# k and v in whole-batch loads and a first stage in another order, in an attention and token-mixing kernel on one NeuronCore

## The chip, the cores and the metric

The kernel runs on one core of a Trainium2 chip. The metric is the device time of one launch in microseconds (us). The core has a matrix engine (TensorE, PE in the profile, with its weight loads shown as PEld), a vector engine (VectorE, DVE), a scalar engine (ScalarE, ACT), a general engine (GpSimd, POOL) and a queue engine (SyncE, SP) that here only starts transfers (DMA). Each engine takes its instructions in program order and waits on semaphores for others.

## The reference

Inputs are float32: q, k, v with 8 batches, 8 heads, 576 rows and 64 columns, a gain `g_norm`, and four weight matrices.

```python
kv = np.einsum('bhsd,bhse->bhde', k, v)
out = np.einsum('bhsd,bhde->bhse', q, kv)
rms = np.sqrt(np.mean(out * out, axis=-1, keepdims=True) + 1e-06)
x = out / rms * g_norm                 # then heads side by side: (8, 576, 512)
...
xt = x.transpose(0, 2, 1)
h = np.maximum(xt @ w_tok1, 0.0) @ w_tok2        # 576 -> 256 -> 576 over rows
u = x + h.transpose(0, 2, 1)
h2 = np.maximum(u @ w_ch1, 0.0) @ w_ch2          # 512 -> 1536 -> 512 over columns
return u + h2
```

The weights arrive as 64-bit numbers; the kernel turns them into float32 itself.

## The kernel before

*Stages.* The batches are worked in four pairs. For each pair there is an attention stage and a token-mixing stage, and these are interleaved: while pair p is mixed, the attention of pair p+1 runs beside it. After the four pairs come the two large channel products, which hold PE for most of the time and which the change leaves alone.

*Order.* Nothing is scheduled by the compiler: every instruction is recorded in program order (`keep`), and the order is written out by hand in lists of short names (`start`, `middle`, `steady`, lines 1241 on) which `play` runs from left to right. `start` is the first stage: the attention of pair 0, the decoding of the token weights, and the first half of the token mixing of pair 0 (batch 0). `middle` follows: the rest of it, for batch 1, and the attention of pair 1. Each name adds instructions to one or several engines; each engine then sees only its own, in that order. The names:

- `kv{s}{h}`: the 64x64 products of k and v for side s (batch) of the pair and half h of its eight heads, 20 matmuls into `ps_kv`. `e{s}{h}` copies them to SBUF (`kvp`), on DVE in pair 0, on ACT later.
- `a{c}{t}`: tile t of chunk c is attended, four 128x128 matmuls into `ps_o` (two buffers). Chunks 0 and 1 are batch 0, chunks 2 and 3 batch 1, chunk 4 is the remainder of 64 rows of both. From pair 1 on an attend is `a{c}`, made of 64x64 matmuls.
- `g`, `q`, `t` for the same tile: gain (DVE multiplies `ps_o` by `g_norm` into x), square (ACT, from `ps_o` to `sq`), total (DVE sums the squares by head). A square follows its gain, since both read the bank, and the bank is free for the next attend after the square.
- `m`, `r`, `i` for a chunk: mean (DVE), root (ACT), inverse (four small DVE instructions).
- `s`, `p`, `d` for a tile: x times the inverse, on ACT (eight instructions of 64 columns), on POOL (one instruction of 512) or on DVE (one of 512). All three are there to choose from.
- `h{s}{t}`: the first token product for side s and half t of the 256 outputs, four 128x512 matmuls into `ps_h`; `h0{t}{j}` is one of these four, for row tile j. `hr` adds the remainder rows. `u{i}` is the second token product.
- `w{n}1` to `w{n}4`: decoding of token weight block n: ACT scales both halves of each number, DVE clamps, shifts and adds. Blocks 0 and 1 are the two halves of `w_tok1`, 2 its remainder rows, 3 and 4 `w_tok2`.
- `l`, `lq`, `lr`: loads of k and v, of q, of q's remainder rows for a later pair.
- `j{n}`: n matmuls of the identity with itself, into a bank that nobody reads (`keep_warm`).

*Loads.* `load(n)` brings half the heads of one batch of k and of v: 512 rows in 128x4 pieces of 256 columns (1 KB each), and 64 rest rows. There are four buffers of k and four of v, so a pair fills all of them. The first two loads of v start on ACT's queue, all others on SP's. Eight semaphores serve the loads on SP and ACT in turn, so a transfer waits until the one eight issues ahead of it has landed. Ahead of `start`, in this order: load 0, the two halves of the token weights, load 1, q of batch 0, loads 2 and 3, q of batch 1, the remainders, the other token weights.

Of the kernel before, what the change touches and what calls it, by code (L numbers as in the profile page):

```python
# [11 lines left out]
F32 = mybir.dt.float32  # L12
# [8 lines left out]
def kernel(  # L21
# [32 lines left out]
    nc = tc.nc  # L54
    P = 128
    B, S, DM = k.shape
    D = g_norm.shape[0]
# [3 lines left out]
    J, JJ, HF = 4, 5, 64  # L61
    LO = P * J
# [3 lines left out]
    DH = DM // 2  # L66
# [11 lines left out]
    def pool(name, bufs, side="left", stack=ctx, **kw):  # L78
        return stack.enter_context(tc.tile_pool(name=name, bufs=bufs, side=side,
                                                reuse_waits="tile", **kw))  # L80
# [9 lines left out]
    inp = pool("inp", 1, "left", left)  # L90
# [12 lines left out]

    w_ch1 = w1p.tile([P, 4, 4, FQ], F32, name="w_ch1")
    w_ch2 = w2p.tile([P, 4, NS, DH], F32, name="w_ch2")
    k_in = [inp.tile([P, JJ, DH], F32, name=f"k_in{i}") for i in range(4)]
    v_in = [inp.tile([P, JJ, DH], F32, name=f"v_in{i}") for i in range(4)]
    kvp = [inp.tile([P, HP, P], F32, name=f"kvp{i}") for i in range(2)]
    u_rest = dram.tile([J * P, DM], F32, name="u_rest")
    u_rows = lambda u: u_rest if u == B else out[u, :LO]  # L110
# [1 line left out]
    def do(f, *a, **kw):  # L112
        return lambda: f(*a, **kw)
# [6 lines left out]
    def dma(o, i, engine=nc.sync):  # L120
        keep(engine.dma_start(o, i))
# [10 lines left out]
    def matmul(*a, **kw):  # L132
        keep(nc.tensor.matmul(*a, **kw))  # L133
# [1 line left out]

    qT, q_rest = {}, {}

    def load(n):

        if n >= 2 * B:  # L140
            return
        cols = [t[n // 2, :, ts(n % 2, DH)] for t in (k, v)]

        queues = (nc.sync, nc.scalar if n < 2 else nc.sync)
        for dst, c, e in zip((k_in[n % 4], v_in[n % 4]), cols, queues):
            dma(dst[:, :J], c[:LO].rearrange("(j p) e -> p j e", p=P), e)
            dma(dst[:HF, J], c[LO:], e)

    def load_q(b):
        if b < B:  # L150
            qT[b] = qtp.tile([P, HP, LO], F32, name="qT", tag="qT", bufs=2)
            dma(qT[b], q[b].rearrange("(c p) s -> p c s", p=P)[..., :LO])
# [69 lines left out]
    def get_ch2(f):  # L222

        a = 2 * (2 * f // NS)

        def loads(raw):
            t = raw.rearrange("p (h f n) w -> p f h n w", h=2, f=2)
            rows = words(moe_w_ch2)[ts(f, 2 * P)].rearrange("(f p) (h n) w -> f p h n w", f=2, h=2)
            return [(t[:, i], rows[i]) for i in range(2)]

        dst = w_ch2[:, a:a + 2, ds(2 * f % NS, 2)]
        return block(2 * DM, loads, dst.rearrange("p h f n -> p h (f n)"))
# [121 lines left out]
    def attention(pair, groups):  # L354
# [7 lines left out]
        whole = pair == 0  # L362

        def kv(side, half):
            n = 4 * pair + 2 * side + half
            kk, vv = k_in[n % 4], v_in[n % 4]
            if whole:
                o = kv_ps[side, half] = zeroed[half]
            else:
                o = kv_ps[side, half] = ps["kv"].tile([P, 2, P], F32, name="ps_kv", tag="kv")  # L370
            for i in range(2):
                for j in range(JJ):
                    for h in range(2):
                        at = ds(i * P + h * D, D)
                        matmul(o[ds(h * D, D), i, ds(h * D if whole else 0, D)], lhsT=kk[:, j, at],
                               rhs=vv[:, j, at],
                               start=(j == 0), stop=(j == JJ - 1), skip_group_check=True)
# [130 lines left out]
        steps = {}  # L508
        for s in range(2):
            for h in range(2):  # L510
                steps |= {f"kv{s}{h}": do(kv, s, h), f"e{s}{h}": do(evict, s, h),
                          f"l{s}{h}": do(load, 4 * pair + 4 + 2 * s + h)}
            steps |= {f"lq{s}": do(load_q, 2 * pair + 2 + s), f"lr{s}": do(load_q_rest, 2 * pair + 2 + s)}
        for c in range(5):
            if whole:
# [676 lines left out]
    def play(lines, after={}, **stages):  # L1192
# [3 lines left out]
        for name in " ".join(lines).split():  # L1196
# [5 lines left out]
            else:  # L1202
# [6 lines left out]
    channel = ([get_ch1(c, f) for f in range(2) for c in range(NC)]  # L1209
               + [get_ch2(f) for f in range(NF // 2)])  # L1210
    load(0)
    for block in tok1[:2]:
        block[0]()
    load(1)
    for t in [t for pair in zip(k_in, v_in) for t in pair]:
        keep(nc.gpsimd.memset(t[HF:, J], 0.0))
    zeroed = [ps["kv"].tile([P, 2, P], F32, name="ps_kv", tag="kv") for _ in range(2)]
    for t in zeroed:
# [5 lines left out]
    make_identity(nc, ident)  # L1224
    dma(g_sb, bass.AP(tensor=g_norm.tensor, offset=g_norm.offset,
                      ap=[[0, P], [0, 1], list(g_norm.ap[0])]), nc.scalar)
    load_q(0)
    for n in range(2, 4):
        load(n)
    load_q(1)  # L1230
    load_q_rest(0)
    load_q_rest(1)
    for block in tok1[2:] + tok2:
# [5 lines left out]


    start = [
        "kv00 e00 l00 j14 w01 w11 w02 w03 w04 w12 w13 w14", "kv01 j10 e01 l01",
        "a00 g00 q00", "a01 g01 q01 t00", "a10 g10 q10 t01 m0 r0", "a11 g11 q11 t10 i0 p00 p01",
        "kv10 j6 t11 m1 r1 e10 i1 s10 p11", "kv11 j2 e11", "h000 h001 h002 h003", "a20 g20 q20", "a21 g21 q21 t20",
        "h010 t21 m2 r2", "a30 g30 q30 i2 p20", "a31 g31 q31 t30", "h011 t31 m3 r3 p21", "a40 i3 p30 g40 q40 p31",
        "h012 h013 t40 m4 r4 w21 i4 s40 lq0 l10 l11 lr0 lr1"]
    middle = [
        "kv00 e00 w31 w22 w23 w24", "h10 -lq1 w32 w33 w34", "kv01 e01 w41 w42",
        "h11 w43 w44", "hr l00", "a0 q00 g01 q01 g00 t00 t01", "u0 z2 f0", "u1 l01",
        "a1 q10 g11 q11 g10 t10 t11 m0 r0 lq0", "u2 i0", "kv10 e10 z4 d00", "u3 s01", "kv11 e11",  # L1250
        "u4 z6 f1", "a2 q20 g21 q21 g20 s10", "u5 t20 t21 f2", "a4 q40 g41 q41 g40 lr0 lr1 1", "u6 t40 t41 1 l10",
        "a3 q30 g31 q31 g30 lq1 d11", "u7 t30 t31 m2 r2 1 i2 p20 p21 s30", "u8 1 l11 d31"]
    steady = [[
        "kv00 kv01 e00 e01 1 -d40 f3", "h00 1 x00", "h01 1 f4 b00", "a0 q00 g01 q01 g00 l00 1",
        "h10 t00 t01 1 x01", "h11 l01 1 x10 b01", "hr 1 x11 z2 f5 f6", "a1 q10 g11 q11 g10 lq0", "kv10 kv11 e10 e11 t10 t11 m0 r0",
        "u0 i0 1", "u1 1 d00 l10", "u2 s01 z4 1 f7", "a2 q20 g21 q21 g20", "u3 s10 t20 t21",
        "u4 z6 l11", "a4 q40 g41 q41 g40 lr0 lr1 1", "u5 d11 t40 t41 1", "a3 q30 g31 q31 g30 lq1",
        "u6 t30 t31 m2 r2 i2 d20 p21 s30", "u7 1 d31 1", "u8 1 b10 b11"], [
        "kv00 kv01 e00 e01 1 -d40 f8", "h00 1 x20", "h01 1 f9", "a0 q00 g01 q01 g00",
        "h10 t00 t01 1 x21", "h11 1", "hr 1 z2 f10", "a1 q10 g11 q11 g10", "kv10 kv11 e10 e11 t10 t11 m0 r0",  # L1260
# [2 lines left out]
        "u6 t30 t31 m2 r2 i2 d20 p21 s30", "u7 1 d31 b20 b21", "u8 f13"]]  # L1263

    attentions = [attention(0, ((0,), (1,), (2,), (3,), (4,)))]
    attentions += [attention(p, ((0, 1), (2, 3, 4))) for p in range(1, B // 2)]

    mixings = [token_mixing(p, (2, 4, 6)) for p in range(B // 2 - 1)]
# [135 lines left out]
```

## The time and the profile before

| what | us |
|---|---|
| median of 3 runs | 789.2 (789.14 to 789.29) |
| the profiled execution, its own time | 788.88 |
| its span, first to last instruction | 787.1 |
| PE busy | 774.4 (98%) |
| DVE, ACT, POOL busy | 612.9, 265.4, 78.3 |
| moved by DMA | 192.12 MB, mean 244 GB/s |

The profile is one execution of the program. It gives for each engine which instruction ran when, what it waited for, and how long a transfer took from its issue to its landing. The time of a launch is about 1.8 us longer than the span in it. In the profile's names `ps_kv<-v_in,k_in` is a kv product, `ps_o<-kvp,qT` an attended tile, `ps_h<-x,w_tok` a first token product, `ps_j<-ident` the identity products. One float32 matmul appears as two records. Instructions of helper functions carry the helper's line: L133 is `matmul`, L121 `dma`.

How far transfers lie apart at the start: load 0, started at 0.75 us, lets the first kv begin at 6.24; the q of batch 0, started at 7.5, lands 9.1 us later.

### The profile page before, as it was taken

The page shows a single profiled execution, that of the slowest core. Times are in us where ns is not written, and L with a number is a line of the kernel's source. Part 1 is how long each engine was busy: PE and PEld are TensorE (multiplying, and loading weights), DVE is VectorE, ACT ScalarE, POOL GpSimd, SP SyncE. Part 2 cuts the span into 40 slices and gives each one's busy share as a digit, 9 for nine tenths or more (in the row PEclk, how much of TensorE's full clock was granted, in tenths as well). Part 3 has the DMA queues.
Part 4 walks back from the last instruction along what each step waited for, and adds up shares of the span by engine and source line. Part 5 has one row for each costly group of instructions (what it writes and reads, how often), then busy time and mean ns, then how long its engine had stood idle before and what let it go on. Part 6 is the DMA issues. An engine that isn't in the chain of part 4 may idle for free.

```text
span 787.1 us, 14853 instructions
## 1 busy us (share of the span) xinstructions
PE 774.4 (98%) x5832; PEld 652.6 (83%) x5832; DVE 612.9 (78%) x906; ACT 265.4 (34%) x513; POOL 78.3 (10%) x91
## 2 busy tenths in 40 slices
PE   6999999999999999999999999999999999999998
PEld 5655555544888888999988899998889999889998
DVE  2666887796776868988778889776898885787977
ACT  2356564846110133511133242123352113325211
POOL 1211212122410000010100001010000101000111
PEclk9999999999999999999999999999999999999999
DMA  9999999587699795599897579889559889655864
GB/s 295 327 334 371 361 371 344 212 268 282 235 292 337 269 339 148 154 309 205 246 236 231 151 218 272 247 203 290 148 158 283 206 222 230 200 153 151 200 173 91
DMA packets 132614, 192.12 MB, mean 244 GB/s; under 512 B 13633, under 2 KB 92225, under 8 KB 132545
## 3 DMA queue, kind: packets, MB, share of 16 engines
q1 hardware_dynamic: 115984, 167.54, 68.1%
q0 software_dynamic: 14656, 22.02, 13.7%
q10 hardware_dynamic: 1904, 1.61, 0.7%
q8 instruction: 46, 0.75, 0.4%
q14 instruction: 24, 0.19, 0.1%
HBM read 138.31 MB, written 52.82 MB: 243 GB/s over the span
## 4 chain that ended last, share of the span: by engine, by line
PE 95%; DVE 2%; ACT 1%; DMA 1%; issue 0%; SPq 0%; ACTq 0%
PE ps_d L133 28%; PE ps_b L133 19%; PE ps_a L133 19%; PE ps_h L133 8%; PE ps_u L133 8%; PE ps_v L133 5%; PE ps_c L133 3%; PE ps_kv L133 2%; PE ps_w L133 2%; PE ps_o L133 2%; DMA raw<-in_moe_w_tok_dram 1%; ACT x L498 1%; DVE x L444 0%; DVE ms L465 0%; PE ps_j L133 0%
## 5 line engine op out<-in xcount | busy, mean ns | idle before, releaser
L133 PE MATMUL ps_d<-ui,w 128*128 128x256 f32 x504 | 118.6, 379 | 0.0
L133 PEld LDWEIGHTS ps_d<-ui,w 128*128 128x128 f32 x504 | 95.1, 190 | 12.8 <-DVE v L124 0.2
L130 ACT COPY ps_d<-ps_a 128x768 f32<-128x768 f32 (+1 forms) x56 | 32.0, 571 | 215.6 <-PE ps_a L133 215.6
L124 DVE TENSOR_TENSOR v<-v,v 128x1536 f32<-128x1536 f32 (+2 forms) x70 | 103.5, 1483 | 0.3
L133 PE MATMUL ps_b<-w,sv 128*128 128x128 f32 x672 | 84.7, 276 | 0.0
L133 PE MATMUL ps_a<-w,v 128*128 128x128 f32 x672 | 84.2, 275 | 0.0
L133 PEld LDWEIGHTS ps_a<-w,v 128*128 128x128 f32 x672 | 79.9, 192 | 0.2
L133 PEld LDWEIGHTS ps_b<-w,sv 128*128 128x128 f32 x672 | 79.5, 192 | 0.2
L133 PE MATMUL ps_u<-h,w_tok 128*128 128x512 f32 (+1 forms) x160 | 67.2, 606 | 0.2
L133 PE MATMUL ps_d<-w,v 128*128 128x128 f32 x528 | 66.3, 275 | 0.0
L133 PE MATMUL ps_h<-x,w_tok 128*128 128x512 f32 (+1 forms) x160 | 65.5, 603 | 0.7 <-ACT x L498 0.7
L133 PEld LDWEIGHTS ps_d<-w,v 128*128 128x128 f32 x528 | 62.7, 192 | 0.3
L127 ACT ACTIVATE v<-v 128x768 f32<-128x768 f32 (+1 forms) x54 | 42.6, 821 | 55.1 <-DVE v L124 55.1
L133 PE MATMUL ps_d<-w,sv 128*128 128x128 f32 x480 | 60.1, 275 | 0.0
L133 PEld LDWEIGHTS ps_d<-w,sv 128*128 128x128 f32 x480 | 57.1, 192 | 0.2
L133 PEld LDWEIGHTS ps_h<-x,w_tok 128*128 128x128 f32 (+1 forms) x160 | 26.1, 189 | 32.7 <-issue 29.0
L1121 POOL DMA_DIRECT2D out_dram<-us x11 | 14.1, 1278 | 379.3 <-ACT us L130 347.4
L133 PEld LDWEIGHTS ps_u<-h,w_tok 128*128 128x128 f32 (+1 forms) x160 | 24.8, 179 | 31.0 <-issue 25.6
L133 PE MATMUL ps_a<-uT,w 128*128 128x256 f32 x192 | 46.7, 379 | 0.0
L444 DVE TENSOR_TENSOR x<-ps_o,g_sb 128x512 f32<-128x512 f32 x32 | 21.6, 687 | 28.6 <-PE ps_o L133 23.3
L133 PE MATMUL ps_b<-ui,w 128*128 128x256 f32 x168 | 40.8, 379 | 0.0
L133 PEld LDWEIGHTS ps_a<-uT,w 128*128 128x128 f32 x192 | 36.3, 190 | 4.8
(145 smaller groups left out, 1216.2 us busy)
## 6 DMA issues: line engine op xcount, KB each, us to landing
w<-parts SPq DMA_DIRECT2D x168, 384.0 KB, 4.1
w<-parts SPq DMA_DIRECT2D x56, 192.0 KB, 3.4
uT<-blocks SPq DMA_DIRECT2D x36, 256.0 KB, 5.7
k_in<-in_k_dram SPq DMA_DIRECT2D x16, 512.0 KB, 8.7
qT<-in_q_dram SPq DMA_DIRECT2D x8, 1024.0 KB, 9.2
out_dram<-x POOLq DMA_DIRECT2D x16, 512.0 KB, 6.1
v_in<-in_v_dram SPq DMA_DIRECT2D x14, 512.0 KB, 8.8
raw<-in_moe_w_ch_dram SPq DMA_DIRECT2D x8, 768.0 KB, 10.4
```

What stands on the lines that cost most here:

```text
L124: keep(engine.tensor_tensor(out=o, in0=a, in1=b, op=op))
L127: keep(nc.scalar.activation(o, a, AF.Relu))
L130: keep(nc.scalar.copy(o, a))
L133: keep(nc.tensor.matmul(*a, **kw))
L444: keep(nc.vector.tensor_mul(x, bank[c, h], g_sb.to_broadcast([P, number(c), D])))
L498: keep(nc.scalar.activation(x[:, k, h], x[:, k, h], AF.Copy, scale=inv[:, k, h]))
L1121: keep(nc.gpsimd.dma_start(to.rearrange("t p e -> p t e"), a, accum_op=ALU.add))
```

## The change

k and v are loaded for whole batches, in pieces of 512 columns (2 KB), into two buffers each; `l{s}` replaces `l{s}0` and `l{s}1`, and kv picks its half inside the buffer. q of batch 0 is loaded right after k of batch 0, in front of the token weights; only v of batch 0 is on ACT's queue. The list `start` is new: both kv of batch 0 come first, the identity products are 6 and 14 instead of 14, 10, 6 and 2, the token weights are decoded between the gains of the first tiles, tiles are scaled by DVE (`d`) and ACT (`s`) where POOL (`p`) did seven of nine, and kv of batch 1 comes after the first token products. In `middle`, `h10` stands ahead of `kv00`.

```diff
-    k_in = [inp.tile([P, JJ, DH], F32, name=f"k_in{i}") for i in range(4)]
-    v_in = [inp.tile([P, JJ, DH], F32, name=f"v_in{i}") for i in range(4)]
+    k_in = [inp.tile([P, JJ, DM], F32, name=f"k_in{i}") for i in range(2)]
+    v_in = [inp.tile([P, JJ, DM], F32, name=f"v_in{i}") for i in range(2)]
...
-    def load(n):
-
-        if n >= 2 * B:
-            return
-        cols = [t[n // 2, :, ts(n % 2, DH)] for t in (k, v)]
-
-        queues = (nc.sync, nc.scalar if n < 2 else nc.sync)
-        for dst, c, e in zip((k_in[n % 4], v_in[n % 4]), cols, queues):
-            dma(dst[:, :J], c[:LO].rearrange("(j p) e -> p j e", p=P), e)
-            dma(dst[:HF, J], c[LO:], e)
+    def load(b):
+
+        if b < B:
+            for t, dst, queue in ((k, k_in, nc.sync), (v, v_in, nc.sync if b else nc.scalar)):
+                dma(dst[b % 2][:, :J], t[b, :LO].rearrange("(j p) e -> p j e", p=P), queue)
+                dma(dst[b % 2][:HF, J], t[b, LO:], queue)
...
         def kv(side, half):
-            n = 4 * pair + 2 * side + half
-            kk, vv = k_in[n % 4], v_in[n % 4]
+            kk, vv = k_in[side], v_in[side]
...
-                        at = ds(i * P + h * D, D)
+                        at = ds(half * DH + i * P + h * D, D)
...
-                steps |= {f"kv{s}{h}": do(kv, s, h), f"e{s}{h}": do(evict, s, h),
-                          f"l{s}{h}": do(load, 4 * pair + 4 + 2 * s + h)}
+                steps |= {f"kv{s}{h}": do(kv, s, h), f"e{s}{h}": do(evict, s, h)}
+            steps[f"l{s}"] = do(load, 2 * pair + 2 + s)
...
     load(0)
+    load_q(0)
     for block in tok1[:2]:
         block[0]()
-    load(1)
...
-    load_q(0)
-    for n in range(2, 4):
-        load(n)
+    load(1)
     load_q(1)
...
     start = [
-        "kv00 e00 l00 j14 w01 w11 w02 w03 w04 w12 w13 w14", "kv01 j10 e01 l01",
-        "a00 g00 q00", "a01 g01 q01 t00", "a10 g10 q10 t01 m0 r0", "a11 g11 q11 t10 i0 p00 p01",
-        "kv10 j6 t11 m1 r1 e10 i1 s10 p11", "kv11 j2 e11", "h000 h001 h002 h003", "a20 g20 q20", "a21 g21 q21 t20",
-        "h010 t21 m2 r2", "a30 g30 q30 i2 p20", "a31 g31 q31 t30", "h011 t31 m3 r3 p21", "a40 i3 p30 g40 q40 p31",
-        "h012 h013 t40 m4 r4 w21 i4 s40 lq0 l10 l11 lr0 lr1"]
+        "kv00 e00 kv01 e01 j6", "a00 w01 g00 q00", "a01 w02 w03 g01 q01 t00 w04 w11 t01 m0 r0",
+        "a10 g10 q10 i0 d00 d01", "a11 w12 w13 g11 q11 t10 w14", "j14 h000 h001 t11 m1 r1 l0", "h010 h011 i1 d10 s11",
+        "kv10 e10 kv11 e11", "h002 h012 a20 g20 q20", "a21 g21 q21 t20 h003 h013 t21 m2 r2 lq0", "a30 g30 q30 i2 d20 s21",
+        "a31 g31 q31 t30 t31 m3 r3", "a40 g40 q40 i3 s30 d31 t40 m4 r4 w21 i4 s40 l1 lr0 lr1"]
     middle = [
-        "kv00 e00 w31 w22 w23 w24", "h10 -lq1 w32 w33 w34", "kv01 e01 w41 w42",
-        "h11 w43 w44", "hr l00", "a0 q00 g01 q01 g00 t00 t01", "u0 z2 f0", "u1 l01",
+        "h10 w31 w22 w23 w24 -lq1", "kv00 e00 w32 w33 w34", "kv01 e01 w41 w42",
+        "h11 w43 w44", "hr l0", "a0 q00 g01 q01 g00 t00 t01", "u0 z2 f0", "u1",
...
```

In the rest of `middle` and in `steady`, `l0` stands where `l00` stood, `l1` where `l10` stood or two products ahead of it, and `l01` and `l11` are gone.

## The prediction

> **What bounds the kernel now.** I read the busy table first, then who TensorE (PE) waits for, then the timeline of its first 52 us, then the stretches of the span.
>
> The page, then PE's waits over the whole span (engine, line, releaser; us in total, times, longest):
>
> ```profile
> span 787.1 us, 14853 instructions
> PE 774.4 (98%) x5832; PEld 652.6 (83%) x5832; DVE 612.9 (78%) x906; ACT 265.4 (34%) x513; POOL 78.3 (10%) x91
> PE   6999999999999999999999999999999999999998
> ...
> PE ps_kv L133 <- DMA v_in<-in_v_dram: 6.2, 1, 6.2
> PE ps_kv L133 <- DVE w_tok L178: 1.1, 1, 1.1
> PE ps_o L133 <- ACT sq L448: 0.8, 2, 0.5
> PE ps_h L133 <- ACT x L498: 0.7, 1, 0.7
> ```
>
> PE is the bound, and of its 12.7 us of idleness the 6.2 before the first matmul is half. The page's first slice (6, then 9s) says the same: all that can be won or lost lies at the start. Stretches (length, then busy time of PE, PEld, DVE, ACT, POOL, clock, DMA share, GB/s):
>
> ```profile
> 2.50:6.24 3.74, 0.00 (x1) 0.03 (x1) 0.00 (x0) 1.49 (x2) 0.79 (x4) 1.00 1.06 331
> ...
> 13.98:16.59 2.61, 2.61 (x53) 2.54 (x50) 1.39 (x3) 0.00 (x0) 0.00 (x0) 1.00 1.06 375
> ...
> 46.05:127.00 80.95, 80.59 (x1049) 42.75 (x1046) 63.68 (x126) 49.96 (x121) 13.73 (x17) 1.00 1.07 361
> ...
> 500.00:787.10 287.10, 283.85 (x1989) 268.21 (x1987) 230.28 (x298) 79.90 (x141) 18.11 (x15) 1.00 0.75 198
> ```
>
> From 46.05 to 500 PE is idle for 0.5 us; the 3.25 missing in the last stretch is the end of the kernel, which the change does not touch. DMA is full in the same first 127 us, but PE does not wait for it after the first loads. So the prediction is one number: when PE reaches the first attend of pair 1 (51.60), from which its queue is full. PE's timeline:
>
> ```profile
> 6.24 2.40 PE L133 MATMUL ps_kv<-v_in,k_in 128*64 128x64 f32 x40 [6.24 <-DMA v_in<-in_v_dram]
> 8.57 4.07 PE L133 MATMUL ps_j<-ident 128*128 128x128 f32 x28
> 13.77 1.39 PE L133 MATMUL ps_kv<-v_in,k_in 128*64 128x64 f32 x40 [1.14 <-DVE w_tok L178]
> 15.09 2.50 PE L133 MATMUL ps_j<-ident 128*128 128x128 f32 x20
> 17.42 1.95 PE L133 MATMUL ps_o<-kvp,qT 128*128 128x128 f32 x16
> ...
> 31.22 1.95 PE L133 MATMUL ps_o<-kvp,qT 128*128 128x128 f32 x16
> 33.00 1.02 PE L133 MATMUL ps_h<-x,w_tok 128*128 128x512 f32 x2
> 33.86 1.95 PE L133 MATMUL ps_o<-kvp,qT 128*128 128x128 f32 x16
> 35.65 1.02 PE L133 MATMUL ps_h<-x,w_tok 128*128 128x512 f32 x2
> ...
> 39.79 1.39 PE L133 MATMUL ps_kv<-v_in,k_in 128*64 128x64 f32 x40
> 41.10 3.70 PE L133 MATMUL ps_h<-x,w_tok 128*128 128x512 f32 x8
> ```
>
> Start to start this prices everything on PE: a kv of 20 matmuls (40 records) 1.31 us, the first one 2.33; one attended tile 0.89; one 128x512 product 0.91; a dummy record 0.117 (20 in 2.33).
>
> And the scaling on ACT:
>
> ```profile
> 27.33 2.02 ACT L498 ACTIVATE x<-x,inv 128x64 f32<-128x64 f32 x8 [1.28 <-DVE inv L484]
> ```
>
> **What the Trainium skill says.** "TensorE: Matmul & The Clock Gate", Part 1, has the array at half clock until some 3.4 us of activity, and again after an idle window of that length. The trace agrees with the first half: 2.33 against 1.31, and the dummies are slow until about 10.0, so 3.8 us; no gap in it is long enough to show the second half. The same page (its paragraph on engine queue depths) says ACT and DVE queues are strictly in order; the timelines show nothing else. "VectorE: DVE Perf Modes", section on the TRN2 errata, charges every small instruction a fixed latency: the eight 64-column scalings cost 2.02, one 512-column multiply on DVE 0.69. "DMA: Bandwidth & Descriptors", "Issuing engines are not separate DMA queues": SP's and ACT's transfers share 16 engines, so two doubled loads at once take twice as long.
>
> **The change part by part.** All times below are a schedule by hand with the durations above, instructions in the order that the built program of the changed kernel has.
>
> *Whole-batch loads.* The first kv needs 1.05 MB before (main parts of half k and half v), 2.10 after. The extra 1.05 MB takes 2.8 us at 375 GB/s (a stretch in which a q load of 2 KB rows moves), and 2 KB rows save some of the first part (331 to 375: 0.4). First matmul at about 6.24+2.8-0.4, taken as 8.5; bounds 7.5 and 9.2. Later loads are wider and half as many; they lie beside a full PE, so they are worth nothing, and their buffers (two where there were four halves) are refilled after the second half is read, 20 us or more before use. SP has 30 issues fewer (60 to 30); PE does not wait for its issue time. POOL's eight clearings of 0.31 become four of twice the width, done before 4, ahead of the first kv.
>
> *kv00 and kv01 together.* Slow for 3.8 us: 2.33 + 1.47 slow, rest 0.5, to 12.8; six dummies (1.4) to 14.2. q, now in front of the token weights, has 1.05 MB behind 2.36: lands near 12, hidden by these. First attend at 14.2 instead of 17.42: 3.2 won, and 12 of 32 dummies gone.
>
> *First tiles.* DVE's gain of a tile starts 1.1 after its attend, ACT's square follows it (0.69, 0.60), and only then is the bank free. g00 15.3 to 16.0; a10 waits for its square, 16.7. DVE now decodes token weights between the gains (w02 w03, 0.9), so g01 ends at 17.6, its square at 18.25, a11 18.3 to 19.2. Fourteen dummies (3.3) to 22.5. Token weights land near 13.5 and 15.2 (0.52 MB each at 310 GB/s), before ACT reads them.
>
> DVE in order: t00, w04, t01, m0 to 19.7 (0.65+0.69+0.65+0.18); g10 20.35; i0 (root and four small ops) 21.35; d00 and d01, which POOL did in 2.04, 0.7 each to 22.7; w12 w13 23.6; g11 24.25; t10 24.9; w14 25.5. The second token product waits for w14 in the built program: h000 22.5 to 23.4, then 2.1 idle, to 25.55. POOL's scaling stood beside DVE; here decode and scaling queue on DVE: that is the first loss.
>
> *Middle of the stage.* h001 h010 h011 28.3; kv10 kv11 30.9 (their loads land near 21: slack); h002 h012 32.7; a20 a21 34.5, at which the kernel before was at 33.0 (31.22+1.78). The gain of 3.2 is spent. h003 h013 36.3; a30 a31 38.1.
>
> *The last wait.* g20 to 34.5, its square and g21, q21 36.05, t21 36.8, m2; g30 holds DVE to 38.1; i2 39.0; s21 on ACT 39.05 to 41.05. q31, the square of tile 31, was ready at 40.4 but is queued behind these eight scalings: 41.05 to 41.6. t31 42.3, m3 and root 42.85, g40, i3 44.15, s30 44.2 to 46.2. PE meanwhile: remainder 39.8, h10's first product 40.7, second (after s21) 41.95, third needs s30: idle 4.3 to 46.25. Before, the like chain from a31 (about 35.6) to the end of POOL's p31 (42.57) is 6.9 long; mine is 8.1, and h10 now stands ahead of kv00, so kv00 and kv01 (2.6) no longer cover it.
>
> *Sum.* h10's last two 1.8: 48.05; kv00 kv01 50.7; h11 3.6: 54.3; the four remainder products 1.9: 56.2. Before 51.60. Later by 4.6, and nothing after it has idle time to absorb this. Ledger: start +2.3, slow part of the second kv +0.7, dummies 4.7 for 8.3, so -3.6, wait for w14 +2.1, last wait +4.3, short waits (a10, a11 and the remainder 0.7 each, s21 0.3) +2.4, waits of before -3.5 (the 2.6 listed, and about 0.2 at each of the five that the modelled end of the matmul ahead hides): 4.7, the same within rounding.
>
> The execution profiled took 788.88 for a span of 787.1; the median shown is 789.2. 787.1+4.6 is a span of 791.7, a time of 793.5 on that execution and 793.8 on the median.
>
> **Rivals.** *Slower still:* the 4.3 us of idleness ends in half clock, as the skill has it for a window of 3.4; price as at the start, 3.8 us of half-speed work, 1.9: 795.7. Against it: an idle stretch barely over the window need not fill one.
> *No difference:* the last wait is short, because squares and scalings interleave better than I lay out or s30 comes before PE gets there: 793.8-4.3 = 789.5. For it: before, such chains end just in time; against it, 6.9 measured.
> *Faster:* the 3.2 us won at the first attend stay won. It needs both waits, 2.1 and 4.3, filled, deciding where w14 ends before 23.4 and s30 before 42: 793.8-6.4 = 787.4. For it: 3.6 us of dummies less and the earlier attend are sure; against it, DVE's list from 14.2 to 25.5 has under 1 us of slack.
> *The wider rows do something later:* PE's 0.5 us of waits between 46 and 500 is all they can win.
>
> **How the numbers follow.** Slower by my chain 0.67, by it with half clock 0.18, no difference 0.08, faster 0.07. This kernel's measurement tells 0.2%, 1.6 us, from no change. So slower 0.85, same 0.08, faster 0.07. Predicted 793.8. Range: first load from 7.5 to 9.2 moves it by -1.0 to +0.7, handovers of some 0.05 over about 20 steps by another 1, half clock by +1.9: 791.6 to 796.6; the cases left out hold under 0.2.
>
> **What would show it.** First matmul 8 to 9; first attend near 14; waits of PE for the token decode (about 2) and for ACT's x scaling in the last products of pair 0 (about 4, releaser L493 in the changed file); DMA GB/s higher up to 127 us without effect; the first 64x64 attend near 56. I am wrong if that attend stands at or before 52, or if PE has new gaps after it.

## The result, and the profile after

| | before | after |
|---|---|---|
| median, us | 789.2 | 798.85 (796.74 to 799.39) |
| ratio of after to before | | 1.0114, 95% interval [1.0098, 1.013] |
| span of the profiled execution, us | 787.1 | 797.1 |
| PE busy, us | 774.4 | 774.6 |
| DVE, ACT, POOL busy, us | 612.9, 265.4, 78.3 | 615.7, 269.5, 71.2 |
| first kv, first attend, a0 of pair 1, us | 6.24, 17.42, 51.60 | 11.83, 18.15, 61.66 |

The change makes the kernel slower by 1.1%, about twice what was predicted, and outside the range. The new 10 us of the span are all there when PE reaches a0 of pair 1, 10.06 later than before. From there to the end both kernels take the same 735.4 to 735.5 us (length of the stretch first; the changed kernel's line stands below, with its other stretches). The kernel before:

```profile
51.60:787.10 735.50, 731.77 (x5410) 621.68 (x5408) 586.84 (x841) 246.94 (x468) 68.35 (x70) 1.00 0.81 239
```

PE's timeline of the changed kernel (start and length in us, engine, line, operation, records, and in brackets the idle time ahead with its releaser):

```profile
11.83 4.63 PE L133 MATMUL ps_kv<-v_in,k_in 128*64 128x64 f32 x80 [11.83 <-DMA v_in<-in_v_dram]
16.39 1.92 PE L133 MATMUL ps_j<-ident 128*128 128x128 f32 x12
18.15 1.95 PE L133 MATMUL ps_o<-kvp,qT 128*128 128x128 f32 x16
...
23.01 3.29 PE L133 MATMUL ps_j<-ident 128*128 128x128 f32 x28
26.13 1.02 PE L133 MATMUL ps_h<-x,w_tok 128*128 128x512 f32 x2
28.86 2.84 PE L133 MATMUL ps_h<-x,w_tok 128*128 128x512 f32 x6 [1.71 <-DVE w_tok L174]
31.64 2.55 PE L133 MATMUL ps_kv<-v_in,k_in 128*64 128x64 f32 x80
...
42.99 2.33 PE L133 MATMUL ps_h<-x,w_tok 128*128 128x512 f32 x4
49.11 3.78 PE L133 MATMUL ps_h<-x,w_tok 128*128 128x512 f32 x4 [3.79 <-ACT x L493]
52.82 3.35 PE L133 MATMUL ps_kv<-v_in,k_in 128*64 128x64 f32 x80
56.11 5.62 PE L133 MATMUL ps_h<-x,w_tok 128*128 128x512 f32 x16
61.66 1.16 PE L133 MATMUL ps_o<-kvp,qT 64*64 64x64 f32 x64
```

The first kv begins 5.6 us later, yet the first attend only 0.7 later, since six identity products stand ahead of it where there were 24. The rest is lost between first attend and a0 of pair 1, which takes 43.5 us where it took 34.2.

PE's waits over the whole span of the changed kernel (releaser; us in total, times, longest):

```profile
PE ps_kv L133 <- DMA v_in<-in_v_dram: 11.8, 1, 11.8
PE ps_h L133 <- ACT x L493: 3.8, 1, 3.8
PE ps_h L133 <- DVE w_tok L174: 1.7, 1, 1.7
PE ps_o L133 <- ACT sq L443: 1.0, 3, 0.5
PE ps_r L133 <- ACT sq L443: 0.6, 1, 0.6
```

Between first attend and a0 of pair 1 these are 6.8 us: 3.79, 1.71, 0.58, and 0.76 of the waits for `sq`, whose third comes later. Before, the waits in the same place were 1.4:

```profile
19.89 2.05 PE L133 MATMUL ps_o<-kvp,qT 128*128 128x128 f32 x16 [0.52 <-ACT sq L448]
...
29.40 1.98 PE L133 MATMUL ps_h<-x,w_tok 128*128 128x512 f32 x4 [0.73 <-ACT x L498]
...
36.85 1.09 PE L133 MATMUL ps_r<-kvp,qR 128*64 128x128 f32 x16 [0.18 <-ACT sq L448]
```

The stretches around the longest wait (length, busy time of PE, PEld, DVE, ACT, POOL, granted clock, DMA share, GB/s), again of the changed kernel:

```profile
42.99:49.11 6.12, 2.25 (x6) 0.59 (x4) 4.69 (x12) 4.51 (x18) 0.00 (x0) 0.89 1.07 334
49.11:52.82 3.71, 3.71 (x4) 1.18 (x4) 1.72 (x8) 3.44 (x13) 0.00 (x0) 0.50 1.10 316
52.82:56.11 3.29, 3.29 (x82) 3.22 (x81) 1.58 (x3) 0.78 (x2) 0.00 (x0) 0.73 0.22 82
56.11:61.66 5.55, 5.55 (x21) 2.13 (x17) 1.68 (x3) 2.13 (x4) 0.00 (x0) 1.00 0.81 247
61.66:797.10 735.44, 731.72 (x5410) 621.76 (x5408) 586.95 (x841) 247.04 (x468) 68.57 (x70) 1.00 0.80 237
```

PE is "busy" in the second and third line, but at a clock of 0.50 and 0.73. Two token products last 3.71 us there, where two at full clock start 1.82 apart (34.12 to 35.94 in the same timeline). Two kv last 3.29 instead of 2.48. So 2.7 us went into half clock, and no wait shows them: they must be read from the clock, or from the length of work that is known. The trace holds every change of the granted clock: in this execution it was at one half from 47.80 to 54.62. The 5.5 us of that in which PE was working again, from 49.11 on, cost half of themselves.

The 10.06 us, added up: first attend 0.7 later; 5.4 more of waits; 2.7 of half clock; 0.8 more of identity products behind the first attend (3.12 us against 1.73 and 0.55). That is 9.6. Most of the rest is inside the line from 42.99, whose two products take 2.33 where two take 1.98 elsewhere; the waits list doesn't show it.

The end of the longest wait is the chain that was laid out by hand, here on ACT in the changed kernel (L443 is the square, L493 the scaling, L470 the root), then two lines of DVE (L497 is the scaling d20, L439 the gain of tile 31):

```profile
41.32 0.60 ACT L443 ACTIVATE sq<-ps_o 128x512 f32<-128x512 f32 x1 [0.84 <-DVE x L439]
42.12 2.02 ACT L493 ACTIVATE x<-x,inv 128x64 f32<-128x64 f32 x8 [0.21 <-DVE inv L479]
44.05 0.57 ACT L443 ACTIVATE sq<-ps_o 128x512 f32<-128x512 f32 x1
45.58 0.21 ACT L470 ACTIVATE root<-ms 128x16 f32<-128x16 f32 x1 [0.96 <-DVE ms L465]
46.24 0.60 ACT L443 ACTIVATE sq<-ps_r 128x512 f32<-128x512 f32 x1 [0.44 <-DVE x L439]
47.04 2.02 ACT L493 ACTIVATE x<-x,inv 128x64 f32<-128x64 f32 x8 [0.21 <-DVE inv L479]
```

```profile
42.12 0.69 DVE L497 TENSOR_TENSOR x<-x,inv 128x512 f32<-128x512 f32 x1
42.73 0.69 DVE L439 TENSOR_TENSOR x<-ps_o,g_sb 128x512 f32<-128x512 f32 x1
```

The gain of tile 31 (42.73) stands behind the scaling d20 on DVE, its square (44.05, with no idle ahead of it) behind the eight scalings s21 on ACT, and s30, from 47.04, is what PE waits for until 49.11.

### The profile page after: what moved, and what is told of

Same layout as the page of the kernel before. It is cut to its first block, busy times and chain, and to the rows that moved or that the text cites. A ratio compares the mean times of both kernels' runs of the same rounds, so it can differ in the third digit from the quotient of the medians.

```text
span 797.1 us, 14751 instructions
## 1 busy us (share of the span) xinstructions
PE 774.6 (97%) x5808; PEld 651.6 (82%) x5808; DVE 615.7 (77%) x911; ACT 269.5 (34%) x529; POOL 71.2 (9%) x80
## 4 chain that ended last, share of the span: by engine, by line
PE 95%; DVE 2%; DMA 1%; ACT 1%; issue 0%; ACTq 0%
PE ps_d L133 28%; PE ps_b L133 19%; PE ps_a L133 19%; PE ps_h L133 8%; PE ps_u L133 8%; PE ps_v L133 5%; PE ps_kv L133 3%; PE ps_c L133 3%; PE ps_w L133 2%; PE ps_o L133 2%; DMA v_in<-in_v_dram 1%; ACT x L493 1%; DVE x L439 1%; DVE ms L460 0%; PE ps_j L133 0%
## 5 line engine op out<-in xcount | busy, mean ns | idle before, releaser
L133 PE MATMUL ps_h<-x,w_tok 128*128 128x512 f32 (+1 forms) x160 | 67.7, 616 | 5.6 <-ACT x L493 3.8
L1116 POOL DMA_DIRECT2D out_dram<-us x11 | 14.2, 1292 | 381.1 <-ACT us L130 260.7
L439 DVE TENSOR_TENSOR x<-ps_o,g_sb 128x512 f32<-128x512 f32 x32 | 21.6, 688 | 26.6 <-PE ps_o L133 21.3
```

Of the source, the lines that this page charges most:

```text
L439: keep(nc.vector.tensor_mul(x, bank[c, h], g_sb.to_broadcast([P, number(c), D])))
L1116: keep(nc.gpsimd.dma_start(to.rearrange("t p e -> p t e"), a, accum_op=ALU.add))
```

## The experiments

Twelve kernels ran. "Gain" below compares ratios: the changed kernel is at 1.0114, which is 9.0 us over the kernel before; the intervals reach 0.6 to 2.1 us to either side. In the table, times are of the profiled execution (first kv, first attend, a0 of pair 1), then median and ratio to the kernel before.

| run | first kv | first attend | a0 of pair 1 | median | ratio, 95% |
|---|---|---|---|---|---|
| x1_loads_only | 11.96 | 21.95 | 56.11 | 794.4 | 1.0074 [1.0047, 1.0101] |
| x2_order_only | 6.52 | 15.78 | 58.88 | 795.79 | 1.0084 [1.0069, 1.0099] |
| x7_loads_less_idle_work | 11.35 | 17.65 | 53.59 | 791.9 | 1.0033 [1.0023, 1.0044] |
| x5_rows8k | 9.08 | 15.29 | 58.72 | 797.01 | 1.0092 [1.0074, 1.0111] |
| x6_one_queue | 11.62 | 17.14 | 59.61 | 798.57 | 1.0109 [1.0088, 1.013] |
| x12_q_behind_k | 11.11 | 17.60 | 61.25 | 797.92 | 1.0108 [1.0095, 1.0121] |
| x3_kv_ahead | 12.16 | 18.15 | 56.38 | 793.21 | 1.005 [1.0035, 1.0065] |
| x4_warm | 11.38 | 17.43 | 58.34 | 796.75 | 1.0097 [1.0082, 1.0112] |
| x8_pool_scaling | 11.52 | 17.46 | 55.69 | 793.3 | 1.0046 [1.0028, 1.0063] |
| x9_all_three | 9.48 | 15.01 | 51.35 | 789.06 | 0.9999 [0.9991, 1.0007] |
| x11_repaired_filled | 6.42 | 14.04 | 54.09 | 789.85 | 1.0013 [1.0004, 1.0021] |
| x13_filled_8k | 9.45 | 15.00 | 52.15 | 787.53 | 0.9984 [0.9973, 0.9994] |

### The two parts apart

**x1_loads_only**: the kernel before with whole-batch loads, in its own order.

```diff
-    for n in range(2, 4):
-        load(n)
+    load(1)
...
-        "kv00 e00 l00 j14 w01 w11 w02 w03 w04 w12 w13 w14", "kv01 j10 e01 l01",
+        "kv00 e00 j14 w01 w11 w02 w03 w04 w12 w13 w14", "kv01 j10 e01 l00",
```

> Only the loads are changed: whole batches of k and v in the kernel before, with its own order of the first stage. Theory A (most of the loss sits in the order of the stage: the wait for the last scaled tiles, the half clock after it, the wait for the token weights): the first kv starts near 11.8 as in the changed kernel, but the 8.3 us of identity products and q's later place absorb most of it; the first attend comes near 18.5 to 19 (17.42 before), so 790 to 791.5 us. Theory B (the loads are the cause): the 5.6 us by which the first kv is late go through to the end, 794 to 796 us.

**x2_order_only**: the order and scaling of the changed kernel, with half-batch loads and four buffers each.

```diff
     load(0)
+    load(1)
     load_q(0)
...
-    load(1)
+    for n in range(2, 4):
+        load(n)
```

> Only the order is changed: the changed kernel with k and v loaded in halves, four buffers each, q of batch 0 still in front of the token weights. Theory A: first kv near 6.3, second half and q land near 12 and 14.5, first attend near 15.5; the waits for the token weights (about 1.7) and for the last scaled tiles (about 3.8, with half clock behind it, 2.6) stay, so 795.5 to 797 us. Theory B: with the loads of before back, the time is that of before within 1.5 us, 788 to 790.7.

Each part alone costs most of the whole: 5.8 and 6.6 us, and together they are 9.0. My expectation for the loads alone, that the identity products would take up the late load, was wrong. Not all of that run's loss lies in the first stage: in its profile a0 of pair 1 is 4.5 us late and the end of the span 5.9. Of the 1.4 in between, 1.2 is one wait of PE for DVE in the channel products (`ps_d` for `v`), which neither the kernel before nor the changed one has; its cause is open. PE's timeline of x1_loads_only:

```profile
11.96 2.40 PE L133 MATMUL ps_kv<-v_in,k_in 128*64 128x64 f32 x40 [11.96 <-DMA v_in<-in_v_dram]
14.29 4.08 PE L133 MATMUL ps_j<-ident 128*128 128x128 f32 x28
18.30 1.39 PE L133 MATMUL ps_kv<-v_in,k_in 128*64 128x64 f32 x40
19.61 2.50 PE L133 MATMUL ps_j<-ident 128*128 128x128 f32 x20
21.95 1.95 PE L133 MATMUL ps_o<-kvp,qT 128*128 128x128 f32 x16
```

The 24 identity products, 4.0 and 2.3 us from start to start, stand behind the load in PE's queue and run after it, whether anybody needs the pause or not. Filler with a fixed count is no slack. What the order gives back when both parts are together is, at the first attend, that it has 18 of these fewer ahead of it.

**x7_loads_less_idle_work** takes the same 18 out of x1_loads_only.

```diff
-        "kv00 e00 j14 w01 w11 w02 w03 w04 w12 w13 w14", "kv01 j10 e01 l00",
+        "kv00 e00 w01 w11 w02 w03 w04 w12 w13 w14", "kv01 j6 e01 l00",
```

> The kernel with the whole-batch loads alone, with the 14 identity products after the first kv taken out and the 10 after the second cut to 6. In the run with loads alone PE ran them all behind the late first kv (first attend 21.95, q there at 17.97). If it is these that carry the late load to the end: first attend near 18.2, 790.2 to 791 us. If something else waits for the loads: above 792.

First attend 4.3 us earlier, a0 of pair 1 only 2.5 earlier: a wait of 2.35 for v of batch 1 appears ahead of 24.89, where x1_loads_only, which came to this kv at 26.40, had none. The gain is 3.2 us, the time 0.9 over the upper end expected.

### Why the first load is late

**x5_rows8k**: the changed kernel, with four adjacent rows of k and v in one partition, so that a piece is 8 KB and not 2 KB (the sums over rows come out the same in any order).

```diff
-t[b, :LO].rearrange("(j p) e -> p j e", p=P)
+t[b, :LO].rearrange("(p j) e -> p j e", j=J)
```

> The changed kernel, with the rows of k and v of a batch given to partitions four in a row (8 KB in one piece) instead of every 128th (2 KB pieces); the sum over rows is the same. If the size or the pitch of the pieces sets the rate of the first loads (about 300 GB/s where q's ran at 375): first kv near 9.5 to 10.5 instead of 11.8, first attend 1.5 to 2 earlier, 796.5 to 797.5 us. If the rate doesn't depend on it: first kv 11.4 to 12.2, time as the changed kernel.

**x6_one_queue**: v of batch 0 on SP's queue behind k, in place of ACT's.

```diff
-(v, v_in, nc.sync if b else nc.scalar)
+(v, v_in, nc.sync)
```

> The changed kernel, with the v of batch 0 on SP's queue behind its k, so that nothing shares the engines with it. If q and the token weights behind k on SP's queue take a part of the bandwidth while v is still coming on ACT's (3.03 MB had moved when the first kv began, which needs 2.10): first kv near 10, first attend 1 to 1.5 us earlier, 797.3 to 798 us. If v is late for another reason: first kv near 11.8 or later.

**x12_q_behind_k**: q and the token weights behind it are held back until k has landed (POOL clears the rest rows' padding ahead of that).

```diff
             qT[b] = qtp.tile([P, HP, LO], F32, name="qT", tag="qT", bufs=2)
+            if b == 0:
+                keep(nc.gpsimd.tensor_copy(qT[0][:1, 0, :1], k_in[0][:1, 0, :1]))
```

> The changed kernel with q and the token weights held back until k of batch 0 has landed (one element of q's tile is first written by POOL out of k's tile), so that nothing moves beside the 2.36 MB of the first load. If the first kv is late because 0.7 to 0.9 MB of q and weights move beside it, k and v land by 9 to 10, first kv at 9.3 to 10.2, and q, which starts at 9 or so, lands near 13, so that the first attend moves from 18.15 to 15.5 to 16.5 and the time is 796 to 797.5. If it is the rate of the 2 KB pieces alone, first kv stays at 11 or later, q lands after 15, first attend at 18 or later and the time is 798.5 to 800.

The same stretch, from 2.50 to 8.00, in the changed kernel, in x5_rows8k and then in x12_q_behind_k, there followed to the end of the load (columns as above):

```profile
2.50:8.00 5.50, 0.00 (x0) 0.00 (x0) 0.00 (x0) 0.87 (x2) 0.65 (x3) 1.00 0.94 332
```

```profile
2.50:8.00 5.50, 0.00 (x0) 0.00 (x0) 0.00 (x0) 0.78 (x2) 0.65 (x3) 1.00 0.94 376
```

```profile
2.50:8.00 5.50, 0.00 (x0) 0.00 (x0) 0.00 (x0) 0.87 (x2) 0.65 (x3) 1.00 0.96 340
8.00:10.00 2.00, 0.00 (x0) 0.00 (x0) 0.00 (x0) 0.00 (x0) 0.00 (x0) 1.00 0.73 189
10.00:11.50 1.50, 0.39 (x8) 0.42 (x9) 0.00 (x0) 0.00 (x0) 0.17 (x1) 1.00 0.29 31
```

With k and v alone on the DMA engines the first kv still begins at 11.11. With the traffic beside them it began between 11.35 and 12.16 in six executions (the changed kernel, x1, x3, x4, x7 and x8), so that traffic costs 0.2 to 1.1 us of the 3.3 by which I was late, not the bulk. The load in this form costs the bulk. In 2 KB rows it moves 340 GB/s at first and then has a tail in which the 16 engines are on average 73% and then 29% busy.

The Trainium skill says that the engines of one transfer "finish independently" and that it has landed when the last has ("DMA: Bandwidth & Descriptors", on why a DMA increments its semaphore by 16). The trace agrees, and shows what the tail is: it holds 16 landings for each transfer. Those of the main part of v in x12_q_behind_k came, ten of them, from 9.11 to 9.43, and the last six from 9.82 to 11.02; PE began 0.09 later. In the changed kernel they lie between 9.40 and 11.74, in x5_rows8k between 8.10 and 8.99, and for the half load of the kernel before between 5.72 and 6.15. Of the 2.6 us by which x12_q_behind_k begins later than my 8.5, 1.6 lie between the tenth landing and the last: a few engines are late, and PE waits for the last of them.

In 8 KB pieces, with q and the weights beside it, the rate is the 376 GB/s that I had reckoned with. The first kv begins at 9.08, within my bounds and earlier than expected for the run; in x9 and x13, which have the same pieces, at 9.48 and 9.45. In the profiles the first attend comes 2.9 us earlier; by the ratios the gain is 1.7, and the intervals overlap. x6_one_queue tells little of v: k landed alone at 6.67, but v only at 11.49, with DMA at a share of 0.59 between 6 and 8, so the one queue brought a lull of its own.

What makes those engines late stays open. It is not the size of a piece alone: q, also in 2 KB pieces, but 2304 bytes apart in memory and on one queue, landed within 0.6 us (15.03 to 15.61) in x12_q_behind_k, and k on one queue within 1.0 (5.67 to 6.67) in x6_one_queue. In the seven executions that load k and v in 2 KB rows on two queues the landings of v spread over 1.9 to 2.6 us. So the second queue, the place of the rows in memory, or both may be in it, and 8 KB pieces also change which rows an engine carries.

### The last wait and half clock

**x3_kv_ahead**: the two kv in front of h10, as in the kernel before.

```diff
-        "h10 w31 w22 w23 w24 -lq1", "kv00 e00 w32 w33 w34", "kv01 e01 w41 w42",
+        "kv00 e00 w31 w22 w23 w24 -lq1", "kv01 e01 w32 w33 w34", "h10 w41 w42",
```

> The changed kernel, with the two kv products of pair 1 ahead of the first token product of batch 1 at the head of the middle list. Theory A: they fill 2.5 of the 3.8 us wait, PE is then never idle long enough to lose its clock (2.6), so about 5 us less: 793 to 794.5 us. Theory B: the wait only moves to another instruction (their loads, or the same tiles later): within 1 us of the changed kernel, 797.9 to 799.9.

**x4_warm**: 14 identity products in front of h10, so that PE isn't idle.

```diff
-        "h10 w31 w22 w23 w24 -lq1",
+        "j14 h10 w31 w22 w23 w24 -lq1",
```

> The changed kernel, with 14 identity products (3.3 us) in front of the first token product of batch 1, where PE is about to wait. Theory A: the wait's end does not move, but no idle stretch is long enough for the half clock, so 2.6 us less: 796 to 796.8, and the runs lie closer together. If the half clock is not what costs these 2.6 us: 798.5 to 799.5, or later, since the identity products delay the first two products.

**x8_pool_scaling**: the first tiles scaled by POOL and ACT, as in the kernel before.

```diff
-        "a10 g10 q10 i0 d00 d01"
+        "a10 g10 q10 i0 p00 p01"
-        "h010 h011 i1 d10 s11"
+        "h010 h011 i1 s10 p11"
-        "a30 g30 q30 i2 d20 s21"
+        "a30 g30 q30 i2 p20 p21"
-        "a40 g40 q40 i3 s30 d31 t40 m4 r4 w21 i4 s40 l1 lr0 lr1"
+        "a40 g40 q40 i3 p30 p31 t40 m4 r4 w21 i4 s40 l1 lr0 lr1"
```

> The changed kernel, with the eight tiles of batches 0 and 1 scaled as in the kernel before (POOL seven, ACT one, and the remainder). Theory A: DVE is free for the token weights 1.3 us earlier, so that wait goes from 1.7 to about 0.4; the eight ACT instructions ahead of the square of tile 31 and the eight of tile 30 are gone, so the last wait ends 1 to 2 us earlier and is too short for the half clock: 793 to 794.8 us. Theory B (POOL's 1.04 us a tile instead of DVE's 0.69 puts the tiles as late): 797 or more.

PE's timeline of x4_warm, the end of the stage:

```profile
42.28 3.39 PE L133 MATMUL ps_j<-ident 128*128 128x128 f32 x28
45.51 1.88 PE L133 MATMUL ps_h<-x,w_tok 128*128 128x512 f32 x4
48.40 1.99 PE L133 MATMUL ps_h<-x,w_tok 128*128 128x512 f32 x4 [1.00 <-ACT x L493]
50.31 2.55 PE L133 MATMUL ps_kv<-v_in,k_in 128*64 128x64 f32 x80
```

PE stands until the same scaling arrives, and so wins nothing of the wait; it has merely been doing something. But the products behind it run at 1.91 and 2.49 instead of 3.71 and 3.29. That is the half clock by itself: 2.6 us in the trace (the rest of the 3.3 between the two a0 is a first attend 0.7 earlier), 1.3 us by the ratios, whose intervals overlap. The price changes from launch to launch: in x6_one_queue, with the same wait of 3.79, the same work took 2.56 and 3.40, a loss of 1.7. There the clock was at one half for 3.41 us, in the changed kernel's profile for 6.83. The mean granted clock of all executions says the same: of five of the changed kernel three stand at 0.996 (798.85 to 799.39 us) and two at 0.998 (796.74 and 797.10), where 3.41 us at one half are 0.2% of the span; all four of x4_warm stand at 1.000.

x3_kv_ahead and x8_pool_scaling each shorten the wait, and each thereby drops the half clock too. The waits of the latter:

```profile
PE ps_h L133 <- DVE ms L465: 1.5, 1, 1.5
PE ps_h L133 <- DVE w_tok L174: 1.0, 1, 1.0
```

(The first line names DVE's mean, which ended last by the profile; the product needs p30, started on POOL at 44.51, 1.04 long.) Against the changed kernel this is 2.3 less at the last wait and 0.7 less at the token weights. With 2.7 of half clock, 0.7 of an earlier first attend and a new short wait of 0.2 that makes 6.2, and a0 comes 6.0 earlier. From the end of a31 to the product that the chain lets go are 5.7 us (39.94 to 45.61) instead of 7.9. The eight scalings that kept back the square of tile 31 are only 0.6 of these 2.2: the gain of tile 31, no longer behind d20 on DVE, comes 0.7 sooner after a31, and scaling tile 30 takes 1.0 less on POOL than in eight pieces on ACT.

### All together, and a better one

**x9_all_three** is the changed kernel with the edits of x3, x5 and x8.

> The changed kernel with three edits that each took time off by themselves: rows of k and v in pieces of 8 KB, scaling of the first tiles on POOL and ACT as in the kernel before, kv00 and kv01 ahead of h10 in the next list. If the three losses are separate (late first load, scaling, order), first attend at 15.3, first attend to a0 of pair 1 the 38.2 of the POOL scaling alone less the 1.5 of its last wait: a0 at 52 and 789.4 to 790.2, level with the kernel before. If the edits of scaling and of order remove the same 1.5 to 3.8 us of the last wait and the rest of their gain was the half clock only, a0 stays at 53 or later and the time at 790.5 to 791.5.

It is level with the kernel before. The three gains by themselves, 5.1, 1.7 and 5.4 us, sum to 12.2, together they bring 9.1: the last wait and the half clock can be taken away only once. So repairs of first load, scaling and order bring back as much as the change lost.

**x11_repaired_filled** was to beat both. It is x2_order_only with the edits of x3 and x8, and with this:

```diff
-        "kv00 e00 kv01 e01 j6"
+        "kv00 e00 kv01 e01 j2"
...
-        "j14 h000 h001 t11 m1 r1 l0", "h010 h011 i1 s10 p11", "kv10 e10 kv11 e11",
+        "j10 h000 h010 t11 m1 r1 l0", "kv10 kv11 h001 h011 i1 s10 p11 e10 e11",
```

> A version meant to beat both: half-batch loads as before, q right behind them and ahead of the token weights, POOL scaling, kv00 and kv01 ahead of h10, two identity products in place of six after the second kv, and kv10, kv11 and the token product h010 ahead of h001, where PE waits for the decode of the token weights. First attend at 14, when q lands, against 17.42 before; from there to a0 of pair 1 about 35.4 (38.2 with the POOL scaling, less 1.5 for the order, less 1.0 to 1.7 for the filled wait): a0 at 49 to 50 against 51.6, and 787 to 788. If the loads of batch 1 land after 21 and PE waits for them, or DVE's list between the first gain and the decode stretches by what is gained, 789 to 790.

PE's timeline of it, where it failed:

```profile
14.04 2.42 PE L133 MATMUL ps_o<-kvp,qT 128*128 128x128 f32 x16
...
38.58 1.33 PE L133 MATMUL ps_kv<-v_in,k_in 128*64 128x64 f32 x40
42.23 2.35 PE L133 MATMUL ps_kv<-v_in,k_in 128*64 128x64 f32 x40 [2.31 <-DMA v_in<-in_v_dram]
```

Up to 38.58 it is ahead of the kernel before, which begins this kv at 39.79. Then v of batch 2 isn't there, and behind that wait the kv runs at half clock (0.52 in the stretch 42.23 to 44.51). This v was issued at 33.56, 1.9 us later than in the kernel before, and wanted 4.8 us earlier. There its main part had landed at 40.5, with 4.3 us to spare.

**x13_filled_8k** starts from x9_all_three, with the same filling, and the loads of batch 2 ahead of the later token weights:

```diff
-    for block in tok1[2:] + tok2:
-        block[0]()
...
-        "kv00 e00 kv01 e01 j6"
+        "kv00 e00 kv01 e01 l0 wl j2"
...
-        "j14 h000 h001 t11 m1 r1 l0", "h010 h011 i1 s10 p11", "kv10 e10 kv11 e11",
+        "j10 h000 h010 t11 m1 r1", "kv10 kv11 h001 h011 i1 s10 p11 e10 e11",
...
+    more["wl"] = lambda: [block[0]() for block in tok1[2:] + tok2]
```

> The version with the three repairs, in which PE's remaining idleness is filled: two identity products after the second kv in place of six, ten in place of fourteen; h010, kv10 and kv11 ahead of h001, where PE waits for the token weights; and the loads of k and v of batch 2 ahead of the remaining token weights, so that kv00 of pair 1 doesn't wait for them. First attend at 14, when q lands (15.0); h000 at 22.4 (23.0); the wait for the decode filled; a0 of pair 1 at 50 to 50.8 (51.35), 787.6 to 788.6, a ratio under 0.9995 to the kernel before. If a load or the decode of the token weights comes late in its new place, PE waits there and the time is 789 to 790.

At 0.9984 [0.9973, 0.9994] it beats both kernels, by 0.16% and 1.3%. No load is waited for after the first. The first attend, expected at 14, came at 15.00, as in x9_all_three: there PE came to full clock at 12.81, here at 15.21, and that ate what the identity products gave. Its profiled execution took 790.16 us and is not typical of a median of 787.53. Its clock fell although no wait behind the first load was longer than 0.95 us, as it did by their mean clock (0.998) in four of the fourteen executions (789.93 to 791.20); the ten others took 787.08 to 788.28:

```profile
24.00:27.00 3.00, 2.05 (x5) 0.41 (x6) 2.58 (x8) 0.81 (x2) 0.20 (x1) 0.74 1.18 346
27.00:31.00 4.00, 4.00 (x82) 3.67 (x83) 0.99 (x3) 2.02 (x8) 1.04 (x1) 0.77 1.02 334
```

## Why the prediction was right and wrong

- *Direction and place: right.* Slower, all of it before a0 of pair 1, nothing after.
- *Whole-batch loads, 8.5 (7.5 to 9.2): wrong, and the step that failed.* It came at 11.83. The term was 1.05 MB at 375 GB/s, less 0.4 for wider rows. That rate was measured in a stretch with a load of q, whose rows lie otherwise, and was given to k and v for having the same 2 KB; the 0.4 were never seen at all (332 GB/s from 2.50 to 8.00, where the first load of the kernel before had 331). And a mean rate left out that PE waits for the slowest engine: ten of v's sixteen landings were there at 9.82, the last at 11.74. x12_q_behind_k shows 2.6 of the 3.3 us in the load itself, and x5_rows8k, at 376 GB/s, the term as I had it, within its bounds. I held q to be behind the load and put no price on what moves beside it, 0.2 to 1.1.
- *First attend 14.2: wrong by the same term.* 18.15: 3.3 from the load, the rest in the two kv (4.56 for 4.3) and the identity products (1.76 for 1.4): PE was slow for 5.25 us from its first kv (to 17.08), where I had taken over the 3.8 of the kernel before. In x7 it was 2.9, in x13 5.8, so the 3.8 was the chance of one launch. The load's error of 3.3 passes on in full, since all that follows is a chain from the first attend. With 11.83 in place of 8.5, the prediction would have been 797.1.
- *Wait for the token weights 2.1: right*, 1.7. *Last wait 4.3: right*, 3.8, by the chain as laid out: 7.9 long against 8.1.
- *Half clock: placed in a rival at 0.18, and it came.* In the profile it cost 2.7, by the ratios 1.3, against the 1.9 named. I had argued that an idle stretch barely over the window need not fill one. The stretch was even shorter, 3.79 by the profile, and it need not fill one: the clock fell at 47.80, and in the 3.41 us up to then PE had been busy for 0.93. The Trainium skill's figure ("TensorE: Matmul & The Clock Gate", Part 1) is an idle window of about 3.4 us; the trace agrees with the length, not with a window idle throughout. An estimate just above that limit was a reason for the likelier case, not for a small chance.
- *Wider rows later worth nothing: right.* The end, from a0 of pair 1, is 735.44 against 735.50.
- *Sum.* 56.2 was predicted for a0, 61.66 came: 3.95 from the first attend, 2.7 from half clock, less 0.9 of the two waits, less 0.3 elsewhere. Two sums were loose: the upper terms of the range, added to 793.8, give 797.4 and not 796.6, and the 2.6 of listed waits in the ledger hold 0.24 that lie behind the stage (at 71.64).

## What to carry to other kernels

Price a transfer by a stretch in which the same tensor moves in the same pieces, and ask what is the end of its slowest engine, not only its mean rate. When an order is changed, follow each queue in which a ready instruction stands behind a slow one, here a gain behind one scaling and a square behind eight; and where waits leave PE idle for most of 3.4 us, count slow work behind them, 1.7 us here for each 3.41 us of work at half clock. Repairs that remove the same wait don't add up, and an earlier engine can use up the slack of loads behind it.

## What the hardware showed that I had not expected

- A load of k and v in 2 KB pieces on two queues ends in a tail with the DMA engines 29% busy, in which six of the sixteen still land their share, the last of v 1.6 us after the tenth (9.43 and 11.02 in x12_q_behind_k). In 8 KB pieces the first 2.1 MB are there 1.6 to 2.8 us sooner (first kv at 9.08 to 9.48 against 11.11 and 11.83).
- The granted clock changes only at times that lie whole multiples of 3.41 us apart, on a grid that starts elsewhere in each execution: in the changed kernel at 17.08, 47.80 and 54.62, 9 and 2 such steps apart, and so in all fourteen profiles. Half clock behind a wait lasted one step (x2, x6, x11, x13) or two (the changed kernel, x5, x12).
- No step that ended in a fall was idle throughout, as the Trainium skill's idle window of some 3.4 us would have it: in six of seven PE was busy for 0.12 to 0.35 of the step, by the profile. Waits of 3.79 us did it in five profiles, and one of 2.31 us, all of it in one step, in x11_repaired_filled. One of 2.35 us in x7_loads_less_idle_work, of which 0.4 fell into the next step, did not (PE busy for 0.44).
- The busy share isn't the whole rule: two waits of 0.71 and 0.95 us left PE busy for 0.51 of a step in x13_filled_8k, and the clock fell; for 0.54 in x11_repaired_filled, and it stayed, as with 0.49 and 0.50 in x2 to x6. And it can go either way from launch to launch: six of the twelve executions of x7_loads_less_idle_work have a mean clock of 0.996 to 0.998 (792.16 to 794.18 us), six 1.000 (790.90 to 791.63).
